# One piece per partition for the loads of the read-out's queries and of the value tile

## The chip, the cores and the metric

The kernel runs on one core of one Trainium2 chip. The metric is the device time of one execution in microseconds (us); the time before is the median of three runs.

## The reference

Three stages follow each other; the change lies in the first. The first stage is a recurrence over 768 steps, run for 4 batches and 8 heads with a state of 40 x 40 each:

```python
for t in range(S):
    y[:, :, t] = np.einsum('bhd,bhde->bhe', rt, state)
    Sa = np.einsum('bhde,bhe->bhd', state, at)
    state = state * wt[:, :, None, :] - np.einsum('bhd,bhe->bhde', Sa, bt) \
            + np.einsum('bhd,bhe->bhde', vt, kt)
```

`y`, laid out as 4 x 768 x 320, goes through a gated feed-forward block (320 to 1024, a convolution of width 3 along the sequence, a sigmoid gate, back to 320), and that result through four attention experts of which each token uses the best two. All of it is float32 in the reference.

## The kernel before, in words

The recurrence is solved in chunks. The sequence is cut into 12 stretches of 64 tokens (`NT`), each into two steps of 32 tokens (`NC`), so 24 steps `k` run one after the other. The 32 head-and-batch pairs are held as `NP = 8` places times four: two halves `al` (or `a`) and two halves `be` (or `b`, `h`). Half of a tile lies on partitions 0 to 63 and the other half on 64 to 127.

Per stretch `prep` works out decays, scaled keys and a triangular inverse `T`. Per step, `chain(k)` forms the corrected values and the new state, and `post(k)` forms the step's read-out. The feed-forward generator `ff` follows them step by step, and `attention` runs after all 24 steps, from about 600 us on.

Four loads per step matter here, all of them issued on SyncE's queue (SP):

- `load_v(k)` fetches the step's values twice: into `SV` (line 138, two loads of 32 partitions, each partition getting two pieces of 320 floats that land next to each other) and into `VZ` (line 143, four loads of 32 partitions, each partition getting eight pieces of 40 floats).
- `load_ra(k)` fetches the read-out's queries `ra` (line 148, two loads of 40 partitions, each partition getting 16 pieces of 32 floats).
- `load_vt(k)` fetches transposed values into `VT` (line 153, two loads, also 16 pieces of 32 floats per partition).
- `load_rb(k)` fetches the same queries in another arrangement into `RB` (line 158, two loads of 40 partitions, each getting one piece of 512 floats).

`VZ` holds the values on partitions 0 to 31 and 64 to 95, and the corrected values, with a minus sign, on partitions 32 to 63 and 96 to 127. The corrected values are written there from PSUM by ScalarE at line 378. Half `be = 0` is filled on the lower partitions only and half `be = 1` on the upper ones only; the rest stays zero. Sixteen matmuls of `chain` (called at line 385, recorded under the helper's line 163) then use `VZ` as the operand that streams past the keys `KB`, 80 columns each. Four copies on ScalarE (line 396) bring the corrected values into `U`. When all of that is done, `load_v(k + 1)` may overwrite `VZ`.

`ra` is the streaming operand, 64 columns each, of sixteen matmuls in `post` (line 444, also recorded under line 163), against `VT`. There is one buffer each of `SV`, `VZ`, `ra`, `VT` and `RB`, so each load waits until the readers of the step before have finished.

The order: `run` merges the generators into one program order by due times written into their `yield`s. From this program order, the tile framework's planner sets the order on each engine and queue, with modelled times (`schedule_with_timeline_sim=True`). Each engine then runs its own list in order, SP too: an SP load that waits for a semaphore holds back every load listed behind it. Besides the loads named, SP issues the loads of `w`, `a` and `kb` (lines 120, 126, 131), the copies of `F` into `a` (line 233), of `KB` and `S` into `LB` (lines 423, 425), the stores of `xe` into `xs` (line 470), the weight loads of the feed-forward block (line 498) and its output (line 634).

Of the kernel before, what the change touches and what calls it, by code (L numbers as in the profile page):

```python
# [8 lines left out]
F32 = mybir.dt.float32  # L9
# [3 lines left out]
AF = mybir.ActivationFunctionType  # L13
# [8 lines left out]
NP, NC = 8, 2  # L22
# [3 lines left out]
R = (slice(0, 40), slice(64, 104))  # L26
Z = (slice(0, 64), slice(64, 128))
E = slice(0, 104)
# [21 lines left out]
class Kernel:  # L50
# [7 lines left out]
    def setup_a(self, ctx):  # L58
        tc, nc = self.tc, self.nc
        cp = self.cp = ctx.enter_context(tc.tile_pool(name="acst", bufs=1))  # L60
        self.wk = ctx.enter_context(tc.tile_pool(name="awk", bufs=2))
        self.w = cp.tile([128, 32, 32], F32, name="w")
        self.kb = cp.tile([128, 16, 2, 2, 32], F32, name="kb")

        self.a = [cp.tile([128, 2, 2, 16, 32], F32, name=f"a{j}") for j in range(2)]
        self.SV = cp.tile([128, 2, 2, NP, 40], F32, name="SV")
        self.ra = cp.tile([128, NP, 2, 2, 32], F32, name="ra")

        self.LB = [cp.tile([128, 2, NP, 2, 40], F32, name=f"LB{j}") for j in range(2)]
        self.RB = cp.tile([128, 2, NP, 2, 32], F32, name="RB")  # L70
        self.P = [cp.tile([128, 32, 32], F32, name=f"P{j}") for j in range(3)]

        self.U = [cp.tile([128, NP // 2, 104], F32, name=f"U{j}") for j in range(2)]
        self.VZ = cp.tile([128, NP, 2, 2, 40], F32, name="VZ")
        self.VT = cp.tile([128, NP, 2, 64], F32, name="VT")
        self.sT = [cp.tile([128, NP, 104], F32, name=f"sT{j}") for j in range(2)]
        self.S = [cp.tile([128, NP, 2, 40], F32, name=f"S{j}") for j in range(2)]
        self.g21 = cp.tile([128, 8, 2, 16], F32, name="g21")
        self.d1 = cp.tile([128, 8, 32], F32, name="d1")
        self.M1 = cp.tile([128, 8, 2, 16], F32, name="M1")  # L80
        self.po = self.ps[3][:, 1].rearrange("p (a b) -> p a b", a=2)
        nc.vector.memset(self.w[32:64], 1.0)
        nc.gpsimd.memset(self.kb[32:64], 0.0)
        nc.gpsimd.memset(self.a[0][32:64], 0.0)
        nc.vector.memset(self.P[0][:, :, 0:1], 1.0)
        nc.vector.memset(self.po[:, 1], 0.0)
        nc.vector.memset(self.ps[1][:, 1, 256:], 0.0)
        cst = cp.tile([128, 164], F32, name="cst")
        self.ident, self.mask = cst[:, :128], cst[:, 128:160]
        self.m0, self.m1, self.m2 = cst[:, 160:161], cst[:, 161:162], cst[:, 162:163]  # L90
        self.cst = cst
        self.t = {}
        self.work = self.nn = 0
# [39 lines left out]
    def load_v(self, k):  # L133

        nc, i = self.nc, self.i
        for al in range(2):
            o = 64 - 64 * al
            nc.sync.dma_start(self.SV[o:o + 32, al].rearrange("p b u d -> p b (u d)"),
                              i["v4"][k].rearrange("(b a t) x -> a t b x", b=2, a=2)[al])
        for h in range(2):  # L140
            for al in range(2):
                v = i["v4"][k, 64 * h + 32 * al:64 * h + 32 * al + 32].rearrange("p (u d) -> p u d", d=40)
                nc.sync.dma_start(self.VZ[64 * h:64 * h + 32, :, al, h], v)

    def load_ra(self, k):

        for h in range(2):
            self.nc.sync.dma_start(self.ra[R[h], :, :, h], self.i["ra"][k, 40 * h:40 * h + 40].rearrange(
                "p (u b t) -> p u b t", u=NP, b=2))

    def load_vt(self, k):
        for h in range(2):
# [180 lines left out]
    def chain(self, k):  # L333
        nc, wk, t = self.nc, self.wk, self.t[k // NC]
        U, KB, u0 = self.U[k % 2], t["KB"], NP * (k % NC)
        zero = k == 0
        sT, sN = self.sT[k % 2], self.sT[(k + 1) % 2]

        def st(x):
            y = x[E]  # L340
            return bass.AP(tensor=y.tensor, offset=y.offset, ap=[list(y.ap[0]), [104, NP], [64, 2], [1, 40]])

        So, SV = self.S[k % 2], self.SV

        def back(p0):
            Sp = self.ps[3][:, 0].rearrange("p (m x) -> p m x", m=4)
            for p in range(4):
                self.tr(WR, Sp[E, p, :104], sT[E, p0 + p], self.ident[:104, :104])
            nc.scalar.activation(So[E, p0:p0 + 4], Sp[E].rearrange("p m (a e) -> p m a e", a=2)[:, :, :, :40], AF.Copy)

        cu = self.ps[0]
        Xp = cu[:, 0, :320].rearrange("p (m d) -> p m d", m=NP)
        for p in range(NP):
            for al in range(2):
                for be in range(2):
                    q = 32 * (2 * be + al)
                    r = slice(0, 96 + 8 * al)
                    self.mm(XA, Xp[q:q + 32, p], t["a"][r, be, al, u0 + p], SV[r, al, be, p], start=True, stop=True)
            if p == 3:
                yield 0.06  # L360
        X = wk.tile([128, NP, 40], F32, name="X", bufs=1)
        nc.scalar.activation(X, Xp, AF.Copy)
        yield 0.14
        if not zero:
            back(0)
            yield 0.25
        for p in range(NP):
            for al in range(2):
                for be in range(2):
                    q = 32 * (2 * be + al)  # L370
                    s, o = slice(q, q + 32), 64 * be + 32
                    self.mm(WX, cu[o:o + 32, al, p * 40:p * 40 + 40], t["T"][s, u0 + p], X[s, p], start=True, stop=True)
        VZ = self.VZ
        for be in range(2):
            s = slice(64 * be + 32, 64 * be + 64)
            y = VZ[s, :, :, be].rearrange("p m a d -> p a m d")
            z = cu[s, :, :320].rearrange("p a (m d) -> p a m d", m=NP)
            nc.scalar.activation(y, z, AF.Copy, scale=-1.0)
        yield 0.4
        if not zero:  # L380
            back(4)
            yield 0.5
        for p in range(NP):
            for al in range(2):
                self.mm(WD, cu[R[al], p // 4, 80 * (p % 4):80 * (p % 4) + 80], KB[:, u0 + p, al],
                        VZ[:, p, al].rearrange("p b d -> p (b d)"), start=True, stop=True)
        for be in range(2):
            s = slice(64 * be + 32, 64 * be + 64)
            for r in range(2):
                y, z = U[64 * r + 32 * be:64 * r + 32 * be + 32], VZ[s, r::2, :, be]  # L390
                y = bass.AP(tensor=y.tensor, offset=y.offset, ap=[list(y.ap[0]), [104, NP // 2], [64, 2], [1, 40]])
                if UD:
                    for al in range(2):
                        nc.sync.dma_start(U[64 * r + 32 * be:64 * r + 32 * be + 32, :, 64 * al:64 * al + 40], VZ[s, r::2, al, be])
                else:
                    nc.scalar.activation(y, z, AF.Copy)
        qq = t["q0"][E, u0:u0 + NP, :, None].to_broadcast([104, NP, 2, 40])
        for h in range(2):
            ps = slice(4 * h, 4 * h + 4)
            Dv = cu[E, h, :320].rearrange("p (m b d) -> p m b d", m=4, b=2)  # L400
            if zero:
                nc.vector.tensor_tensor(st(sN)[:, ps], Dv, qq[:, ps], op=ALU.mult)
            else:
                nc.vector.tensor_tensor(st(sN)[:, ps], Dv, st(sT)[:, ps], op=ALU.add)
        if not zero:
            nc.vector.tensor_tensor(st(sN), st(sN), qq, op=ALU.mult)
        if k + 1 < NT * NC:
            for al in range(2):
                y = sN[R[al]]
                y = bass.AP(tensor=y.tensor, offset=y.offset, ap=[list(y.ap[0]), [64, 2], [104, NP], [1, 40]])  # L410
                nc.gpsimd.tensor_copy(SV[R[al], al], y) if al < SC else nc.scalar.activation(SV[R[al], al], y, AF.Copy)
        if k + 1 < NT * NC:
            self.load_v(k + 1)
        yield 1.0

    def post(self, k):
        nc, wk, t = self.nc, self.wk, self.t[k // NC]
        n, c = divmod(k, NC)
        P, VT = t["P"], self.VT
        ra, LB, RB, u0 = self.ra, self.LB[k % 2], self.RB, NP * c  # L420
# [19 lines left out]
        for p0 in range(0, NP, 4):  # L440
            ap = po(p0, 0).rearrange("p (u a t) -> p u a t", u=4, a=2)
            for p in range(4):
                for be in range(2):
                    self.mm(WA, ap[64 * be:64 * be + 64, p], VT[E, p0 + p, be], ra[E, p0 + p, be], start=True, stop=True)
            for be in range(2):
                s = slice(64 * be, 64 * be + 64)
                y = RB[s, be, p0:p0 + 4].rearrange("p u a t -> p (u a) t")
# [583 lines left out]
```

## Time and profile before

| | before |
|---|---|
| median of 3 runs | 901.09 us (898.76 to 907.43) |
| the profiled execution | 902.53 us |
| its span, first to last instruction | 900.8 us |
| mean granted TensorE clock | 0.929 |
| TensorE (PE) busy | 756.9 us, 84% |
| VectorE (DVE) busy | 699.4 us, 78% |
| ScalarE (ACT) busy | 571.3 us, 63% |
| GpSimd (POOL) busy | 365.6 us, 41% |

Shares are of the span. DMA-issuing instructions on SP don't count as busy; "SPq" in the chain of waits is time in which the chain runs through SP's issuing. The chain of work that ended last is followed back from the last instruction, at each step to what released it. The span lies 1.7 us below the profiled execution's own time. The 24 steps and the feed-forward block fill about the first 600 us, the attention the rest.

### The profile page before, as it was taken

What the parts mean: (1) busy time and instruction counts of PE and PEld (TensorE: products, weight loads), DVE (VectorE), ACT (ScalarE), POOL (GpSimd) and SP (SyncE); (2) the same over time, 40 slices, a digit from 0 to 9 for tenths busy, and PEclk for the clock granted to TensorE, in tenths of its full rate; (3) what the DMA queues carried; (4) which work ended last, traced back from release to release, by engine and by line L of the source; (5) the groups of instructions that cost most, each with busy time, mean ns of one, the idle gap of its engine ahead of it and who ended that gap; (6) DMA issues with size and microseconds to landing.
All of it is one profiled execution on the core that took longest, in us unless ns stands there. A gap on an engine that the chain in (4) does not pass through costs nothing.

```text
span 900.8 us, 31560 instructions
## 1 busy us (share of the span) xinstructions
PE 756.9 (84%) x13112; PEld 659.8 (73%) x13112; DVE 699.4 (78%) x1614; ACT 571.3 (63%) x1353; POOL 365.6 (41%) x419
## 2 busy tenths in 40 slices
PE   1257667988889988898988889959889989999988
PEld 1156556777778877787877779858778878888876
DVE  6888698798798989899898794656567776786664
ACT  1156556676676748584857577657767666776665
POOL 6163443434333324344333235564434353344353
PEclk9999568998898889998998899979999999999999
DMA  5434574545454556553646355250011100110001
GB/s 128 105 121 115 139 170 106 132 101 136 104 132 113 122 130 146 120 128 77 146 108 152 68 121 118 48 143 28 10 45 37 45 16 31 37 38 16 17 15 37
DMA packets 143488, 81.17 MB, mean 90 GB/s; under 512 B 113858, under 2 KB 127042, under 8 KB 142386
## 3 DMA queue, kind: packets, MB, share of 16 engines
q1 hardware_dynamic: 138450, 74.34, 33.8%
q0 software_dynamic: 4896, 4.83, 2.4%
q8 instruction: 103, 1.69, 0.8%
q14 instruction: 39, 0.32, 0.1%
HBM read 51.63 MB, written 11.80 MB: 70 GB/s over the span
## 4 chain that ended last, share of the span: by engine, by line
PE 38%; DVE 29%; ACT 10%; DMA 9%; issue 6%; POOL 4%; SPq 3%; POOLq 0%; ACTq 0%; DVEq 0%
PE ps L163 8%; PE ps L720 4%; DVE cv L604 4%; PE ps L823 4%; PE ps L569 4%; PE ps L806 4%; PE ps L592 3%; PE ps L167 2%; PE ps L770 2%; DVE RB L448 2%; PE ps L711 2%; DVE Q L200 2%; PE ps L838 2%; PE ps L771 2%; DVE a L211 2%
## 5 line engine op out<-in xcount | busy, mean ns | idle before, releaser
L792 POOL TENSOR_TENSOR A<-A,rs 128x128 f32<-128x128 f32 (+5 forms) x96 | 87.7, 936 | 106.3 <-DVE rs L790 61.3
L607 POOL TENSOR_TENSOR cv<-cv,h 128x512 f32<-128x512 f32 (+1 forms) x48 | 59.1, 1230 | 150.0 <-ACT cv L606 129.0
L604 DVE SCALAR_TENSOR_TENSOR cv<-h,cw,cv 128x256 f32<-128x256 f32 (+1 forms) x192 | 97.1, 546 | 25.0 <-ACT cv L602 21.9
L569 PE MATMUL ps<-xh,win 128*128 128x256 f32 x384 | 94.3, 302 | 5.8 <-ACT xh L545 4.2
L569 PE MATMUL ps<-xl,win 128*128 128x256 f32 x384 | 95.1, 300 | 0.5 <-POOL xl L546 0.4
L592 PE MATMUL ps<-wout,gh 128*128 128x320 f32 x384 | 90.5, 331 | 5.8 <-ACT gh L486 5.5
L777 ACT ACTIVATE A<-ps,nm 128x128 f32<-128x128 f32 (+5 forms) x96 | 60.8, 634 | 35.8 <-DVE nm L775 26.8
L487 POOL TENSOR_TENSOR gl<-cv,gh 128x512 fp32r<-128x512 f32 x48 | 62.6, 1305 | 44.6 <-ACT gh L486 44.0
L569 PEld LDWEIGHTS ps<-xh,win 128*128 128x128 f32 x384 | 71.3, 204 | 7.9 <-ACT xh L545 4.7
L592 PEld LDWEIGHTS ps<-wout,gh 128*128 128x128 f32 x384 | 66.2, 201 | 8.3 <-ACT gh L486 6.8
L569 PEld LDWEIGHTS ps<-xl,win 128*128 128x128 f32 x384 | 70.9, 202 | 1.8 <-POOL xl L546 0.8
L775 DVE TENSOR_REDUCE nm<-ps 128x1 f32<-128x128 f32 (+5 forms) x96 | 58.6, 619 | 16.9 <-PE ps L773 10.8
L163 PE MATMUL ps<-kb,a 40*32 40x64 f32 x1536 | 39.2, 254 | 32.7 <-DVE kb L207 29.4
L592 PE MATMUL ps<-wout,gl 128*128 128x320 f32 x192 | 59.4, 332 | 0.9 <-POOL gl L487 0.9
L163 PE MATMUL ps<-RB,LB 104*40 104x32 f32 (+1 forms) x1536 | 50.6, 213 | 11.1 <-DVE RB L448 6.9
L163 PEld LDWEIGHTS ps<-kb,a 40*32 40x32 f32 x1536 | 30.9, 129 | 37.6 <-issue 19.2
L163 PEld LDWEIGHTS ps<-RB,LB 104*40 104x40 f32 (+1 forms) x1536 | 42.2, 127 | 20.5 <-DVE RB L448 9.0
L720 PE MATMUL ps<-x,wqk 128*128 128x384 f32 x256 | 54.5, 353 | 2.8 <-DVE lg L714 2.4
L606 ACT ACTIVATE cv<-cv 128x512 f32<-128x512 f32 (+1 forms) x48 | 30.3, 630 | 39.8 <-DVE cv L604 39.5
L806 PE MATMUL ps<-cid,A 128*128 128x128 f32 x336 | 53.0, 277 | 2.2 <-POOL A L792 1.5
L770 PE MATMUL ps<-k,q 128*128 128x256 f32 (+3 forms) x144 | 49.5, 352 | 3.6 <-ACT A L777 3.3
L163 PE MATMUL ps<-ra,VT 104*64 104x64 f32 x768 | 43.8, 255 | 8.4 <-DVE RB L448 6.8
(178 smaller groups left out, 2177.7 us busy)
## 6 DMA issues: line engine op xcount, KB each, us to landing
kb<-in_kb_e_dram SPq DMA_DIRECT2D x24, 320.0 KB
LB<-KB SPq DMA_DIRECT2D x48, 160.0 KB
LB<-S SPq DMA_DIRECT2D x46, 100.0 KB
a<-in_a_e_dram SPq DMA_DIRECT2D x24, 160.0 KB
VT<-in_vt_dram SPq DMA_DIRECT2D x48, 80.0 KB
RB<-in_rb_dram SPq DMA_DIRECT2D x48, 80.0 KB
SV<-in_v_dram SPq DMA_DIRECT2D x48, 80.0 KB
VZ<-in_v_dram SPq DMA_DIRECT2D x96, 40.0 KB
```

The costliest lines, as they stand in the source:

```text
L163: self.nc.tensor.matmul(*a, **k)
L487: (eng or self.nc.vector).tensor_tensor(lo, x, hi.bitcast(F32), op=ALU.subtract)
L569: nc.tensor.matmul(hp[:, dd], wt[:, 128 * d:128 * d + 128], x, start=k == 0, stop=k == 7)
L592: nc.tensor.matmul(self.ps[1][:, tb, :DM], x, wt, start=d == 0 and k == 0, stop=d == 7 and k == 2)
L604: nc.vector.scalar_tensor_tensor(y, h[:, dd, :, k:k + nt], self.cw[:, k, d:d + 1], y, op0=ALU.mult, op1=ALU.add)
L607: (nc.gpsimd if GM and st % GM == 0 and st >= GN else nc.vector).tensor_tensor(cv[:, :, :, :nt], cv[:, :, :, :nt], h[:, :, :, 1:1 + nt], o ...
L720: nc.tensor.matmul(pp, self.wqk[:, wk, hl, 128 * m:128 * m + 128], x[:, xk], start=j == 0, stop=j == 7)
L770: nc.tensor.matmul(sp[:, c0:c1], q[:, ce, 128 * j:128 * j + 128], k[:, ce, c0:c1], start=True, stop=False)
L775: nc.vector.tensor_reduce(nm, sp[:, :nk], axis=AX.X, op=ALU.max, negate=True)
L777: nc.scalar.activation(A[:, :nk], sp[:, :nk], AF.Exp, bias=nm, accum_out=sums[:, e:e + 1])
L792: nc.gpsimd.tensor_tensor(A[:, :nk], A[:, :nk], rs[:, e:e + 1].to_broadcast([128, nk]), op=ALU.mult)
L806: nc.tensor.transpose(tp[:, m, e], As[e][:, 128 * (2 * g + m):128 * (2 * g + m) + 128], self.cid)
```

## The change

`ra` and `VZ` get another order of axes. In `ra` the half `h` (the one that a load fills) becomes the outermost axis within a partition, so that the 512 floats that a load brings to a partition lie next to each other. In `VZ` the half `be` becomes the outermost axis, then `al`, then the place; one load per half now brings both `al`, two runs of 320 floats of the source that land side by side. Four loads of `VZ` become two. The two matmul groups read the same numbers as before, but each of their streaming operands is now two runs (2 x 40 floats in `VZ`, 2 x 32 in `ra`) where it was one run of 80 or 64. The write at line 378 and the reads at line 396 follow the new order. A branch under `if UD:` is dropped; `UD` is 0, so it never ran.

```diff
-        self.ra = cp.tile([128, NP, 2, 2, 32], F32, name="ra")
+        self.ra = cp.tile([128, 2, NP, 2, 32], F32, name="ra")
...
-        self.VZ = cp.tile([128, NP, 2, 2, 40], F32, name="VZ")
+        self.VZ = cp.tile([128, 2, 2, NP, 40], F32, name="VZ")
...
         for h in range(2):
-            for al in range(2):
-                v = i["v4"][k, 64 * h + 32 * al:64 * h + 32 * al + 32].rearrange("p (u d) -> p u d", d=40)
-                nc.sync.dma_start(self.VZ[64 * h:64 * h + 32, :, al, h], v)
+            nc.sync.dma_start(self.VZ[64 * h:64 * h + 32, h].rearrange("p a u d -> p a (u d)"),
+                              i["v4"][k, 64 * h:64 * h + 64].rearrange("(a t) x -> t a x", a=2))
...
         for h in range(2):
-            self.nc.sync.dma_start(self.ra[R[h], :, :, h], self.i["ra"][k, 40 * h:40 * h + 40].rearrange(
-                "p (u b t) -> p u b t", u=NP, b=2))
+            self.nc.sync.dma_start(self.ra[R[h], h].rearrange("p u b t -> p (u b t)"), self.i["ra"][k, 40 * h:40 * h + 40])
...
-            y = VZ[s, :, :, be].rearrange("p m a d -> p a m d")
+            y = VZ[s, be]
...
-                        VZ[:, p, al].rearrange("p b d -> p (b d)"), start=True, stop=True)
+                        VZ[:, :, al, p], start=True, stop=True)
...
-                y, z = U[64 * r + 32 * be:64 * r + 32 * be + 32], VZ[s, r::2, :, be]
+                y, z = U[64 * r + 32 * be:64 * r + 32 * be + 32], VZ[s, be, :, r::2].rearrange("p a m d -> p m a d")
...
-                    self.mm(WA, ap[64 * be:64 * be + 64, p], VT[E, p0 + p, be], ra[E, p0 + p, be], start=True, stop=True)
+                    self.mm(WA, ap[64 * be:64 * be + 64, p], VT[E, p0 + p, be], ra[E, :, p0 + p, be], start=True, stop=True)
```

## Rows read from the trace of the kernel before

**Rows 1.** The page: busy time per engine, and the chain's shares by engine.

```profile
PE 756.9 (84%) x13112; PEld 659.8 (73%) x13112; DVE 699.4 (78%) x1614; ACT 571.3 (63%) x1353; POOL 365.6 (41%) x419
PE 38%; DVE 29%; ACT 10%; DMA 9%; issue 6%; POOL 4%; SPq 3%; POOLq 0%; ACTq 0%; DVEq 0%
```

**Rows 2.** Busy time by stretch, with granted clock, DMA share and GB/s last.

```profile
360.00:420.00 60.00, 50.40 (x1197) 45.24 (x1199) 55.15 (x113) 38.81 (x87) 23.42 (x24) 0.98 0.52 121
600.00:900.00 300.00, 279.29 (x2249) 240.37 (x2248) 200.92 (x584) 196.24 (x529) 123.45 (x149) 0.98 0.10 32
```

**Rows 3.** SP's issues by line: min/median/max ns, first and last start us.

```profile
L148 SPq DMA_DIRECT2D ra<-in_ra_dram x48: 763/800/4026, 13.8 to 562.5; - x48
L158 SPq DMA_DIRECT2D RB<-in_rb_dram x48: 281/300/1217, 6.9 to 571.4; - x48
L143 SPq DMA_DIRECT2D VZ<-in_v_dram x96: 560/607/1607, 10.4 to 552.2; - x96
L138 SPq DMA_DIRECT2D SV<-in_v_dram x48: 324/392/1602, 9.1 to 539.5; - x48
L153 SPq DMA_DIRECT2D VT<-in_vt_dram x48: 763/764/3974, 6.1 to 565.5; - x48
```

**Rows 4.** Chain in order of time (start, us, what): the issues of ra.

```profile
124.13 1.58 SPq L148
125.76 0.79 SPq L148
...
281.76 0.84 SPq L148
...
282.65 0.82 SPq L148
...
345.93 0.76 SPq L148
...
346.74 0.76 SPq L148
```

**Rows 5.** The chain again: issues of VT after those of ra, longest one last.

```profile
126.59 0.81 SPq L153
...
347.55 3.52 SPq L153
```

**Rows 6.** The chain again: first and last of four VZ issues, a fifth, its landing.

```profile
425.07 0.61 SPq L143
...
427.06 0.60 SPq L143
...
534.48 0.52 SPq L143
535.00 0.05 issue
535.05 2.19 DMA VZ<-in_v_dram
```

**Rows 7.** Matmuls by tile: min/median/max ns; a scattered streaming operand, then a contiguous one.

```profile
L163 PE MATMUL ps<-O,g x768: 209/228/258, 48.5 to 538.6; 32*32 32x32 f32 x192
L163 PE MATMUL ps<-M,d x768: 184/191/258, 53.3 to 542.1; 32*32 32x32 f32 x192
```

**Rows 8.** ScalarE by line: busy us, mean ns, idle before.

```profile
L378 ACT ACTIVATE VZ<-ps 32x640 f32<-32x640 f32 x48 | 33.4, 697 | 15.8 <-PE ps L163 14.8
L630 ACT ACTIVATE yt<-ps 128x640 f32<-128x640 f32 x12 | 8.4, 698 | 0.6 <-PE ps L592 0.5
L396 ACT ACTIVATE U<-VZ 32x320 f32<-32x320 f32 x96 | 44.9, 468 | 1.6
L362 ACT ACTIVATE X<-ps 128x320 f32<-128x320 f32 x24 | 10.3, 430 | 5.5 <-PE ps L163 5.5
```

**Rows 9.** The page's DMA part: packets by size, and the SP queue's share.

```profile
DMA packets 143488, 81.17 MB, mean 90 GB/s; under 512 B 113858, under 2 KB 127042, under 8 KB 142386
q1 hardware_dynamic: 138450, 74.34, 33.8%
```

**Rows 10.** SP's own waits: us in total, times, longest us.

```profile
SPq L158 <- PE ps L163: 26.5, 14, 5.0
SPq L143 <- PE ps L163: 19.5, 12, 9.3
SPq L148 <- PE ps L167: 9.2, 3, 5.7
```

More of the change, by code (lines that the diff above doesn't have):

```diff
@@ L389, in chain @@
             for r in range(2):
-                y, z = U[64 * r + 32 * be:64 * r + 32 * be + 32], VZ[s, r::2, :, be]
+                y, z = U[64 * r + 32 * be:64 * r + 32 * be + 32], VZ[s, be, :, r::2].rearrange("p a m d -> p m a d")
                 y = bass.AP(tensor=y.tensor, offset=y.offset, ap=[list(y.ap[0]), [104, NP // 2], [64, 2], [1, 40]])
[L392 to L396, printed above, removed]
+                nc.scalar.activation(y, z, AF.Copy)
         qq = t["q0"][E, u0:u0 + NP, :, None].to_broadcast([104, NP, 2, 40])
```

## Prediction

> **What bounds the kernel now.** I read the page's busy times first, then the busy times by stretch, then the chain of waits, then SP's issues and waits. No engine is full: TensorE is busy for 84% of the span and VectorE for 78% [rows 1]. In a stretch in the middle of the 24 steps TensorE works 50.4 of 60 us and VectorE 55.15, and the DMA engines are busy for 0.52 of it; in the attention, after 600 us, the DMA share is 0.10 [rows 2]. The first two thirds are a lockstep of engines, and their length is set by the chain that runs through them. That chain is 38% TensorE, 29% VectorE, 9% transfers and 3% SP's issuing [rows 1]: 3% of 900.8 us is some 27 us. The change touches loads of the first 600 us only, and it touches arithmetic nowhere. So its worth has to be sought in those 3%, in the part of the 9% that belongs to its loads, and against that in what the new operand shapes cost TensorE and ScalarE.
>
> **What the loads cost SP now.** An `ra` issue holds SP for a median of 0.800 us and there are 48; a `VZ` issue holds it for 0.607 us and there are 96 [rows 3]. That is 38.4 + 58.3 = 96.7 us of SP, or 4.0 us for each of the 24 steps; from first to last `ra` load it is 548.7 us [rows 3], so a step takes about 23.9 us.
>
> After the change an `ra` load has the shape of today's `RB` load: 40 partitions, one piece of 512 floats each. Its price is a row: 0.300 us [rows 3]. A `VZ` load has the shape of today's `SV` load: 32 partitions, two source runs of 320 floats that land as one. That price is 0.392 us [rows 3], and there are 48 of them, not 96. New sum: 14.4 + 18.8 = 33.2 us. SP is relieved of 63.5 us, 2.6 us per step. Most of this is hidden, since SP's work lies beside that of TensorE and VectorE and only 27 us of all SP issuing stands on the chain. What counts is where these loads stand on it.
>
> **The `ra` issues on the chain.** There are six pieces, 1.58 + 0.79 + 0.84 + 0.82 + 0.76 + 0.76 = 5.55 us [rows 4]. At 0.30 us each they would be 1.8 us: a gain of 3.75 us. Bounds: 0, if another chain of equal length stands beside it, and 5.55, if the loads leave the chain.
>
> **The `VZ` issues on the chain.** Four in a row, between 0.61 and 0.60 us, about 2.4 us in all, and a single one of 0.52 us [rows 6]. The four become two of 0.392, the one becomes 0.392: 2.4 + 0.52 - 0.78 - 0.39 = 1.7 us gained. Bounds 0 and 2.9. Behind the single one stands the landing of that load, 2.19 us [rows 6]; its bytes stay the same, so I take nothing for it, with a bound of half, 1.1 us.
>
> **The queue behind them.** `VT` stays as it is, and its issue has a median of 0.764 us, yet one on the chain took 3.52 us, straight behind two `ra` issues [rows 3, 5]. An issue that takes four times its median was held up by what was already queued. The two `ra` loads ahead of it bring 2 x 640 pieces now and 2 x 40 afterwards. Bounds: nothing, since `VT` itself makes 640 pieces per load, and 2.75 us (down to the median). It is as near to the one as to the other, so I take half: 1.4 us.
>
> **The transfers.** A step's `ra` and `VZ` loads make 2 x 40 x 16 + 4 x 32 x 8 = 2,304 pieces now, all under 512 bytes, and 2 x 40 + 2 x 64 = 208 after; over 24 steps 55,296 become 4,992. The page counts 113,858 packets under 512 bytes [rows 9], so some 58,600 remain. What this saves the DMA engines is bounded by nothing (the bytes are the same) and by 50,304 packets at the SP queue's mean. That mean is 0.338 x 16 x 900.8 us / 138,450 = 35 ns [rows 9], which gives 1,770 us over 16 engines, 111 us of each or 12 points of the share. Small pieces carry few bytes, so I go near the lower end: the queue's share falls from 33.8% to 30 or 32%. With engines about half busy [rows 2], I take no gain on the chain for it beyond the one above.
>
> **TensorE.** Two groups of 16 matmuls per step, 768 each in all, get a streaming operand of two runs instead of one. No row shows two runs. The nearest rows are a pair of the same size: with 32 single floats apart from each other the median is 228 ns, with 32 side by side 191 ns [rows 7]. The difference, 37 ns for 31 extra jumps, is the upper bound for one extra jump: 1,536 x 37 ns = 57 us of TensorE. The lower bound is nothing. In proportion to the jumps it is 1.2 ns each, 1.8 us in all; with TensorE holding 38% of the chain [rows 1] that is 0.7 us lost. I take that, since one jump in 64 or 80 columns is far nearer to a contiguous read than to a scattered one.
>
> **ScalarE.** The write at line 378 becomes contiguous: 697 ns now, and a contiguous write of 640 floats from PSUM takes 698 ns [rows 8], so nothing changes. The reads at line 396 keep runs of 40 floats: 468 ns against 430 for a contiguous copy of 320 floats from PSUM [rows 8]. At worst the difference moves by as much again, 38 ns x 96 = 3.6 us of an engine that holds 10% of the chain, 0.4 us. I take nothing.
>
> **The sum.** -3.75 - 1.7 - 1.4 + 0.7 = -6.2 us. Against the profiled execution's own 902.5 us (span 900.8 and 1.7 around it) that is 896.3. This execution lies 1.4 us above the median of the runs, 901.09, so the median after should be 895.
>
> **A rule against it.** Four issues of `VZ` at 2.4 us stand on the chain, and the one landing of `VZ` on it took 2.19 us [rows 6]: SP's time is as long as the transfer's. The Trainium skill, "DMA: Bandwidth & Descriptors", section "Issuing engines are not separate DMA queues", says that the sequencer's time to initiate a DMA is usually small relative to the DMA itself. By this rule shorter issuing would be worth next to nothing and the time would stay at 901; these rows disagree with it.
>
> **The rivals.**
>
> *Hidden anyway, 899 to 902.* The relieved 63.5 us are off the chain, and where they are on it a neighbouring chain is as long. For it: in the middle stretch VectorE is busy for 92% [rows 2], so a load that comes 1 us earlier finds VectorE still at work. Against it: eleven pieces of these loads stand on the chain as it is [rows 4, 6]. Chance 0.25.
>
> *The queue was the brake, 884 to 890.* SP runs its list in order, so 2.6 us less per step shortens the delay of every load and copy behind: `LB`, `xs`, `a`, `RB`. All of the issuing of `ra`, `VZ` and `VT` in these rows and the half landing would go: 5.55 + 2.9 + 4.3 + 1.1 = 13.9 us [rows 4 to 6], so 887. For it: the 3.52 us stall. Against it: SPq is but 3% of the chain. Chance 0.24.
>
> *SP stands at a closed door, 906 to 918.* SP already waits for TensorE before `RB`, `VZ` and `ra` loads for 26.5, 19.5 and 9.2 us, up to 9.3 us at a time [rows 10], because their single buffers are still being read. Fewer and shorter loads, planned anew, can put a `VZ` load ahead of work that is ready, `xs` or `LB` copies and the feed-forward input behind them; SP then waits at `VZ` while they are late. The three rows make 55.2 us, 2.3 us per step. It decides from 0.26 us more per step (6.2 / 24, the gain is gone); 0.65 us more, a growth by under a third, makes 895 + 24 x 0.65 = 911. For it: the order on SP is a planned one, and it will differ. Against it: two waits fewer per step, as four `VZ` issues become two. Chance 0.13.
>
> *Two runs are dear, 909 to 920.* If an extra jump costs as much as the scattered operand, 57 us of TensorE at 38% is 22 us: 895 - 0.7 + 22 = 916. It decides from about 10 ns per matmul (1,536 x 10 ns x 0.38 = 5.8 us, the gain). For it: nothing shows a two-run operand. Against it: the proportion above. Chance 0.05.
>
> **How the numbers follow.** My own forecast, 895 with a range of 889 to 899, has 0.33. Within 1% is about what a measurement of this kernel can tell from no change: 892.1 to 910.1. Faster than that: all of the braked queue (0.24) and a quarter of my own case (0.08), together 0.32. Slower: a good half of the closed door (0.08) and nearly all of the dear runs (0.04), 0.12. The rest is 0.56. The range reaches from the braked queue's 884 to the smaller half of the closed door at 910; outside lie a fifth of the former, half of the latter and most of the dear runs, under 0.2. Both signs hold much of it, so my own case's range stands beside it above.
>
> **What would show it.** `ra` issues at a median near 0.30 us and 48 `VZ` issues near 0.39; packets under 512 bytes near 58,600; `ra` and `VZ` matmuls within 5 ns of now; line 378 near 697 ns; SPq on the chain down to 2%, and lines 148 and 143 gone from it or under 1 us a piece. The forecast is wrong if SP's waits for TensorE grow by 16 us or more, if the two matmul groups grow by 10 ns or more, or if the chain through VectorE and TensorE comes out longer although the loads behave as forecast: then the new plan, and not the loads, has set the time.

## The result, and the profile after

The changed kernel takes 915.87 us (median of 4 runs, 912.76 to 917.98) against 902.86 us for the kernel before (4 runs, 898.76 to 907.43). The ratio is 1.0135, with an interval from 1.0091 to 1.0179: it became slower by 1.35%. (Ratios here and below leave out a slower state into which some executions of any of these kernels fall, and aren't the quotient of the medians.) The profiled execution took 915.1 us, of which 913.3 are its span.

The page of the changed kernel (busy time by engine, the DMA packets, the SP queue, the chain's shares by engine), to be held against [rows 1, 9]:

```profile
PE 755.2 (83%) x13112; PEld 659.1 (72%) x13112; DVE 708.0 (78%) x1614; ACT 567.9 (62%) x1351; POOL 372.3 (41%) x419
...
DMA packets 92416, 81.17 MB, mean 89 GB/s; under 512 B 57794, under 2 KB 74050, under 8 KB 91314
q1 hardware_dynamic: 87378, 74.33, 31.1%
...
PE 32%; DVE 31%; ACT 12%; DMA 10%; issue 9%; POOL 5%; SPq 1%; ACTq 0%; DVEq 0%; POOLq 0%
```

TensorE works as long as before and SP's issuing has all but left the chain (3% to 1%), yet the span is 12.5 us longer. Next SP's issues of the loads in the changed kernel (min/median/max ns, first and last start in us), which answer to [rows 3]. Line 147 is `ra` (148 before), line 141 `VZ` (143), line 151 `VT` (153):

```profile
L147 SPq DMA_DIRECT2D ra<-in_ra_dram x48: 281/323/1237, 13.6 to 579.4; - x48
...
L141 SPq DMA_DIRECT2D VZ<-in_v_dram x48: 312/416/1768, 10.2 to 570.9; - x48
...
L151 SPq DMA_DIRECT2D VT<-in_vt_dram x48: 763/822/1100, 6.1 to 581.5; - x48
```

The loads became as short as forecast, and the longest `VT` issue fell from 3.97 to 1.10 us. So the place of the loss is elsewhere. Cutting the time at the first `VZ` matmul of step 10 and at that of step 23 (steps counted from 0) finds it. The busy times by stretch of the kernel before (columns: TensorE, weight loads, VectorE, ScalarE, GpSimd, then granted clock, DMA share, GB/s); first everything between the two cuts, then the feed-forward matmuls of lines 569 and 592 alone, then everything after the second cut:

```profile
282.70:565.10 282.40, 249.36 (x5827) 223.02 (x5823) 240.66 (x490) 197.57 (x435) 104.69 (x113) 0.93 0.52 119
...
282.70:565.10 282.40, 65.72 (x416) 57.58 (x416) 0.93 0.52 119
...
282.70:565.10 282.40, 53.75 (x291) 45.18 (x291) 0.93 0.52 119
...
565.10:900.80 335.70, 307.50 (x2588) 265.79 (x2582) 223.01 (x621) 216.33 (x578) 148.36 (x171) 0.98 0.13 37
```

The same four rows of the changed kernel (the feed-forward lines are now 563 and 586):

```profile
281.90:585.10 303.20, 258.56 (x5895) 231.85 (x5895) 252.03 (x499) 201.77 (x450) 112.48 (x115) 0.92 0.44 111
...
281.90:585.10 303.20, 65.25 (x432) 57.55 (x432) 0.92 0.44 111
...
281.90:585.10 303.20, 65.51 (x313) 54.17 (x312) 0.92 0.44 111
...
585.10:913.30 328.20, 297.84 (x2460) 255.91 (x2460) 213.49 (x607) 207.19 (x554) 141.24 (x165) 0.97 0.12 36
```

Up to step 10 the two are level (281.9 against 282.7 us). Then thirteen steps take 303.2 us where they took 282.4, 20.8 us more. After the second cut the changed kernel is 7.5 us quicker (328.2 against 335.7). That adds up: -0.8 + 20.8 - 7.5 = 12.5 us, the growth of the span. The 20.8 us are two things. TensorE does 9.2 us more work there; the feed-forward matmuls have grown by 65.25 + 65.51 - 65.72 - 53.75 = 11.3 us, that is, some of them were brought forward. And TensorE idles 11.6 us longer (303.20 - 258.56 = 44.6 against 282.40 - 249.36 = 33.0). The first part comes back after the loop, where TensorE has 307.50 - 297.84 = 9.7 us less to do. The idling doesn't come back.

What TensorE waits for between the cuts, kernel before (us in total, times, longest):

```profile
PE ps L163 <- DVE RB L448: 10.7, 9, 2.6
...
PE ps L163 <- DVE T L330: 4.2, 2, 2.4
PE ps L163 <- DVE xe L463: 3.3, 3, 1.7
...
PE ps L167 <- ACT KB L267: 1.2, 4, 0.5
```

And in the changed kernel:

```profile
PE ps L161 <- DVE RB L442: 14.5, 8, 3.7
...
PE ps L165 <- ACT KB L265: 5.8, 7, 1.7
PE ps L161 <- DVE xe L457: 5.7, 3, 2.9
...
PE ps L161 <- DVE T L328: 1.0, 2, 0.6
```

TensorE waits 3.8 us longer for VectorE's write of `RB`, 4.6 us longer for ScalarE's `KB`, 2.4 us longer for `xe`, and 3.2 us less for `T`. These are other engines' arithmetic, none of it touched by the change, and no load of the change is among them. It is what a different order of the same work would look like. In fact 5,943 of the 8,168 places in TensorE's list hold another instruction than before. (The trace has more records than the list has places: a step's 16 matmuls on `VZ` stand in it as 32, so each group of 768 records is 384 matmuls.) The question for the experiments was whether that order is the cause, or whether the loads brought the loss about in some other way.

### The profile page after: what moved, and what is told of

The parts are those of the page before. It is cut to its first block, busy times and chain, and to the rows that moved or that the text cites. A ratio compares the mean times of both kernels' runs of the same rounds, so it can differ in the third digit from the quotient of the medians.

```text
span 913.3 us, 31465 instructions
## 1 busy us (share of the span) xinstructions
PE 755.2 (83%) x13112; PEld 659.1 (72%) x13112; DVE 708.0 (78%) x1614; ACT 567.9 (62%) x1351; POOL 372.3 (41%) x419
## 2 busy tenths in 40 slices
DMA packets 92416, 81.17 MB, mean 89 GB/s; under 512 B 57794, under 2 KB 74050, under 8 KB 91314
## 3 DMA queue, kind: packets, MB, share of 16 engines
q1 hardware_dynamic: 87378, 74.33, 31.1%
## 4 chain that ended last, share of the span: by engine, by line
PE 32%; DVE 31%; ACT 12%; DMA 10%; issue 9%; POOL 5%; SPq 1%; ACTq 0%; DVEq 0%; POOLq 0%
DVE cv L598 6%; PE ps L161 4%; PE ps L714 4%; PE ps L817 4%; PE ps L800 3%; DMA xs<-xe 2%; PE ps L705 2%; PE ps L586 2%; DVE RB L442 2%; DVE a L209 2%; PE ps L764 2%; DMA kb<-in_kb_e_dram 2%; PE ps L563 2%; DVE Q L198 2%; PE ps L832 2%
## 5 line engine op out<-in xcount | busy, mean ns | idle before, releaser
L598 DVE SCALAR_TENSOR_TENSOR cv<-h,cw,cv 128x256 f32<-128x256 f32 (+1 forms) x192 | 96.9, 542 | 35.5 <-ACT cv L596 34.8
L601 POOL TENSOR_TENSOR cv<-cv,h 128x512 f32<-128x512 f32 (+1 forms) x48 | 62.5, 1303 | 144.6 <-ACT cv L600 144.1
L586 PE MATMUL ps<-wout,gh 128*128 128x320 f32 x384 | 95.6, 344 | 2.1 <-ACT gh L480 2.1
L771 ACT ACTIVATE A<-ps,nm 128x128 f32<-128x128 f32 (+5 forms) x96 | 60.8, 634 | 37.4 <-DVE nm L769 28.4
L586 PEld LDWEIGHTS ps<-wout,gh 128*128 128x128 f32 x384 | 69.8, 211 | 4.1 <-ACT gh L480 3.1
L161 PE MATMUL ps<-kb,a 40*32 40x64 f32 x1536 | 37.8, 250 | 32.4 <-DVE kb L205 29.9
L586 PE MATMUL ps<-wout,gl 128*128 128x320 f32 x192 | 62.0, 345 | 0.7 <-POOL gl L481 0.6
L161 PEld LDWEIGHTS ps<-RB,LB 128*40 128x40 f32 (+1 forms) x1536 | 41.1, 125 | 24.6 <-DVE RB L442 11.4
```

Source lines behind the costliest of these rows:

```text
L161: self.nc.tensor.matmul(*a, **k)
L586: nc.tensor.matmul(self.ps[1][:, tb, :DM], x, wt, start=d == 0 and k == 0, stop=d == 7 and k == 2)
L598: nc.vector.scalar_tensor_tensor(y, h[:, dd, :, k:k + nt], self.cw[:, k, d:d + 1], y, op0=ALU.mult, op1=ALU.add)
L601: (nc.gpsimd if GM and st % GM == 0 and st >= GN else nc.vector).tensor_tensor(cv[:, :, :, :nt], cv[:, :, :, :nt], h[:, :, :, 1:1 + nt], o ...
L771: nc.scalar.activation(A[:, :nk], sp[:, :nk], AF.Exp, bias=nm, accum_out=sums[:, e:e + 1])
```

## The experiments

**The tool.** The planner chooses the order of each engine's list anew for each program. To part layout from order, the list of each engine was written out from one kernel and forced on another by edges that only order issue:

```diff
         Kernel(tc, ins, {"out": out}).run()
+        follow(tc, nc, ORDER)
...
+            if was is not None:
+                tc.add_manual_dep(seq[e][n], was.name, info, reason="order")
+            was = seq[e][n]
```

`ORDER` is the list of places per engine. No arithmetic changes.

### Layout and order apart

The changed kernel in the order of the kernel before; its edit is the one above, in the changed kernel:

> Both new layouts and the two new load shapes, but every engine and SP's queue issue their instructions in the order of the kernel before (a VZ load takes the place of the first of the two that it replaces). Theory A, the planner's new order costs the time and the loads by themselves are worth what I forecast: 888 to 901 us, under the kernel before. Rival B, the loads or the two-run operands cost the time whatever the order: 912 to 918 us.

Measured: 900.94 us, ratio 0.9963 [0.9921, 1.0006]. The loss is gone with the order. The same kernel was run once more, in five rounds, to tell half a per cent from nothing:

> New layouts in the order of the kernel before once more, for the size of what the loads are worth when the order stays. My sum of -6.2 us gives a ratio of 0.993 to the kernel before; nothing gained gives 1.000; the earlier run gave 0.996.

Measured: 898.67 us against 904.75, ratio 0.9951 [0.9920, 0.9982]. This version beats both kernels. Its busy time by stretch between the same two cuts:

```profile
276.50:558.80 282.30, 250.77 (x5835) 224.68 (x5825) 240.19 (x490) 198.12 (x436) 106.00 (x113) 0.93 0.48 119
```

And two of TensorE's waits there:

```profile
PE ps L161 <- DVE RB L442: 9.0, 8, 2.6
...
PE ps L165 <- ACT KB L265: 0.4, 1, 0.4
```

The thirteen steps are back at 282.3 us, TensorE's idling at 31.5 us, and the wait for `KB` is down from 5.8 to 0.4 us. The granted clock, 0.93 of full speed here and 0.92 in the changed kernel, is too near to make 20.8 us: if all of TensorE's 258.56 us went with it, 0.01 would be some 2.8 us (an estimate).

The cross-check is the old layouts in the order of the changed kernel (the same edit in the kernel before, with the other list):

> The layouts and loads of the kernel before, issued in the order of the changed kernel (each VZ load as two, one behind the other). Theory A: 914 to 925 us, as slow as the changed kernel or slower by the loads' worth. Rival B: 899 to 905 us.

Measured: 923.74 us, ratio 1.0242 [1.0158, 1.0326]. With the layouts untouched, the new order costs more than the whole change did. The matmuls on `VZ`, by tile, in this kernel (min/median/max ns, first and last start us):

```profile
L163 PE MATMUL ps<-VZ,KB x768: 231/233/357, 63.3 to 595.9; 128*40 128x80 f32 x192
```

Its last `VZ` matmul starts at 595.9 us, later than in any kernel so far. Between the first `VZ` matmul of step 10 and that of step 23 it shows

```profile
283.40:593.90 310.50, 265.70 (x5893) 238.45 (x5894) 251.73 (x497) 202.43 (x449) 112.44 (x115) 0.89 0.47 108
```

The four corners by ratio: old layouts in the old order 1, new layouts in the old order 0.995, old layouts in the new order 1.024, new layouts in the new order 1.0135. The order costs 1.9 to 2.4% with either layout. In the old order the layouts gain 0.5%. In the new order they would gain 1%, but the intervals of the two overlap, and the kernel with the old layouts had a mean granted clock of 0.89 there against 0.92 in the changed kernel: TensorE was busy for 7.1 us longer (265.70 against 258.56) with the same matmuls. So the size of their gain in the new order stays open.

### Each part alone, planned anew

The `ra` part of the diff alone, and the `VZ` part alone, the planner free:

```diff
-        self.ra = cp.tile([128, NP, 2, 2, 32], F32, name="ra")
+        self.ra = cp.tile([128, 2, NP, 2, 32], F32, name="ra")
```

> Only ra's layout and load are changed; the planner orders anew. Rival B: the effects of the two parts add up to some +13 us, so this one lies between 898 and 916 and with the VZ part makes the whole. Theory A: no such sum need come out, as each program has an order of its own; within 890 to 920.

Measured: 919.95 us, ratio 1.0198 [1.0123, 1.0274]. That lies above what the adding of parts allowed (898 to 916).

```diff
-        self.VZ = cp.tile([128, NP, 2, 2, 40], F32, name="VZ")
+        self.VZ = cp.tile([128, 2, 2, NP, 40], F32, name="VZ")
```

> Only VZ's layout and loads are changed; the planner orders anew. Rival B: this and the ra part add up to some +13 us over the kernel before. Theory A: they need not; within 890 to 920.

Measured: 916.19 us, ratio 1.0167 [1.0086, 1.0248]. Each half of the change alone costs as much as the whole, within the intervals. Two costs that belonged to the parts would have had to add up.

### Edits that mean nothing

If a new plan is enough to lose a per cent, an edit that does no harm by itself may lose it too. One kernel loads a table of constants a second time at the start, the other clears three tiles in the reverse sequence:

```diff
+        nc.sync.dma_start(self.cst, self.i["consts"])
```

> The kernel before with one load of the constants issued twice at its start: no layout and no load of the loop is touched, some 0.5 us of work is added before the first step, and the planner orders anew (5,183 of TensorE's 8,168 matmuls get another place in its list). Theory A', the order of the kernel before is an uncommonly good one and nearly any new plan is worse: 908 to 925 us. Rival C, the plan gets worse because of the shorter loads: 898 to 907 us.

Measured: 914.26 us, ratio 1.0155 [1.0093, 1.0218]. 5,183 of TensorE's 8,168 places differ from the kernel before.

```diff
-        for t in (self.SV, self.VZ, self.d1):
+        for t in (self.d1, self.VZ, self.SV):
```

> The kernel before with three memsets of the start in another order: not a load, a layout or an operation more or less; 5,922 of TensorE's 8,168 matmuls get another place in its list. Theory A': 908 to 925 us. Rival C: 898 to 907 us.

Measured: 913.43 us, ratio 1.0119 [1.0033, 1.0205]; 5,922 places differ. The `VZ` matmuls of the kernel with the second load of constants:

```profile
L164 PE MATMUL ps<-VZ,KB x768: 229/233/356, 64.4 to 577.6; 128*40 128x80 f32 x192
```

One more load before the first step can't delay the last step by 11.4 us (577.6 against 566.2) by its own length: the first `VZ` matmul starts only 1.2 us later (64.4 against 63.2). Five programs planned anew (the change, its halves, the two empty edits) lie between 1.0119 and 1.0198. So the order that the planner happened to find for the kernel before is better than the five others seen here.

### Where in the loop, and whether on SP

Three kernels with the new layouts put the two orders one after the other. The old order until step 10 and the new one from there:

> New layouts; the order of the kernel before up to the corrected values of step 10, from there the order of the changed kernel. If the loss is made after step 10, as the traces show (the two run level until there): 912 to 920 us. If it is made before: 898 to 905 us.

Measured: 917.51 us, ratio 1.0180 [1.0117, 1.0244]. The mirror of it, the new order until step 10 and then the old:

> New layouts; the order of the changed kernel up to the corrected values of step 10, from there the order of the kernel before. Loss made after step 10: 897 to 905 us. Loss made before: 911 to 918 us. Both this and its mirror near 908: the loss is spread evenly.

Measured: 896.36 us, ratio 0.9963 [0.9926, 1.0000]. And the old order until step 16, then the new:

> New layouts; the order of the kernel before up to the corrected values of step 16, from there the order of the changed kernel. If the loss of the new order is spread evenly over steps 10 to 23: about 908 us. If it lies in one place between step 10 and 16: 898 to 904 us; after step 16: 912 to 918 us.

Measured: 911.38 us, ratio 1.0073 [1.0033, 1.0113]. The `VZ` matmuls of the first, and of its mirror:

```profile
L161 PE MATMUL ps<-VZ,KB x768: 229/233/356, 62.6 to 587.2; 128*40 128x80 f32 x192
```

```profile
L161 PE MATMUL ps<-VZ,KB x768: 230/233/356, 61.6 to 554.6; 128*40 128x80 f32 x192
```

The new order costs nothing in the first ten steps and everything after them: the last step starts at 587.2 or at 554.6 us, depending on the second part alone. All of these kernels, and the one with the old order throughout, are forced by the same kind of edges, so the forcing isn't what parts them. (The changed kernel's own order wasn't forced on it; old until step 10 and then new comes near it, 917.51 against 915.87 us.)

With the cut at step 16 about half of the loss is left by the ratios (0.995, 1.007, 1.018). 911.38 us lies between the forecasts for an even loss (908) and for a loss after step 16 (from 912 on), and the runs scatter from 903.81 to 916.69. The traces speak for uneven steps. From the first `VZ` matmul of step 16 to that of step 23 the kernel before, the changed kernel and this one show

```profile
423.50:565.10 141.60, 127.85 (x2974) 114.60 (x2972) 116.01 (x236) 101.22 (x223) 54.38 (x58) 0.94 0.52 116
```

```profile
428.30:585.10 156.80, 137.27 (x3138) 123.54 (x3131) 128.35 (x254) 109.17 (x245) 63.44 (x63) 0.93 0.43 109
```

```profile
422.70:584.70 162.00, 138.28 (x3094) 124.77 (x3092) 125.30 (x251) 109.22 (x245) 63.80 (x64) 0.94 0.42 105
```

So 15.2 of the changed kernel's 20.8 us fall on the steps from 16 on, and 5.6 on steps 10 to 15 (146.4 us against 140.8). The profiled execution of this kernel, one of its longest at 915.14 us, has 20.4 us from step 16 on.

The rival of the prediction that named a new plan had placed it on SP. So one kernel took the new order on the four computing engines but SP's list from the old one (346 of 592 places differ):

> New layouts, the order of the changed kernel on TensorE, VectorE, ScalarE and GpSimd, but SP issues its loads and copies in the order of the kernel before (346 of 592 places differ). My rival of the closed door, that SP's new list puts loads that must wait ahead of work that is ready, gives 898 to 905 us. If the loss is in the order of the computing engines: 912 to 919 us.

Measured: 929.69 us, ratio 1.0275 [1.0222, 1.0329]. That is outside both forecasts. SP's old list doesn't bring the time back; with the engines in another order it costs more. Since this kernel, too, mixes lists of two plans, the time alone can't clear SP's new list, and the mirror (old lists on the engines, SP's new one) wasn't run.

The traces speak against it. The work that SP would hold up by this rival includes the stores of `xe` into `xs`, from which GpSimd fetches the feed-forward input. GpSimd does wait longer for them between the cuts, kernel before and changed kernel:

```profile
POOL xd L537 <- DMA xs<-xe: 8.0, 5, 3.6
```

```profile
POOL xd L531 <- DMA xs<-xe: 18.9, 9, 4.7
```

But it isn't SP that is late. From the last write to `xe` to the start of a stretch's first store, the twelve stretches take 6.8 us in all in the kernel before (2.85 us at most) and 1.8 us in the changed kernel (0.53 at most). The stores leave almost as soon as `xe` is there. The copies of `S` into `LB`, too, follow the last write to `S` sooner (133.5 us in sum over 46 copies, against 192.0). What comes late is `xe`, or GpSimd comes early; SP doesn't hold that work back. That leaves the lists of the computing engines, though no run shows them by themselves.

### One that settled little

The recurrence in the old order, with the feed-forward instructions in the places that the new order gives them, was to show whether bringing those forward is the harm:

> New layouts. The instructions of the feed-forward generator stand where the changed kernel's order has them among all others; everything else keeps among itself the order of the kernel before. If the new order is slow because it puts feed-forward work ahead of the recurrence from step 10 on: 911 to 919 us. If it is slow by the order within the recurrence and its preparation: 896 to 904 us. In between: both.

Measured: 974.52 to 1003.51 us in five runs, ratio 1.0779 [1.0676, 1.0883]. That is far above both orders, so the kernel doesn't lie between them and can't say which part of the new order costs what. It shows only how much an order may cost that fits neither plan. Its mirror, and kernels that swap the list of TensorE or VectorE alone, weren't run.

The last start of a `VZ` matmul beside the span of the same profiled execution, over all of these but the last:

| kernel | last `VZ` matmul (us) | span (us) |
|---|---|---|
| before | 566.2 | 900.8 |
| new layouts, old order; the same in five rounds | 555.8; 559.9 | 892.1; 897.1 |
| new layouts, new order until step 10, then old | 554.6 | 889.0 |
| changed kernel | 587.0 | 913.3 |
| old layouts, new order | 595.9 | 920.9 |
| `ra` alone; `VZ` alone | 589.8; 584.6 | 915.2; 915.5 |
| constants twice; tiles cleared in reverse | 577.6; 578.0 | 911.1; 910.4 |
| old order until step 10; until step 16, then new | 587.2; 586.6 | 915.6; 913.3 |
| new order, SP's list from the old one | 602.0 | 928.7 |

Whatever loses time has its last step late, and more so than its span; in the changed kernel that is because part of the delay is work brought forward. The others agree: of 1,344 records of feed-forward matmuls in the trace (lines 569 and 592 before), 316 run after the start of step 23 in the four kernels of the table's first three rows, and 244 to 284 in all of the table's others. The loss doesn't follow their number, though: with 284 left (constants twice) the ratio is 1.0155, with 251 (tiles in reverse) 1.0119.

## Why the prediction was wrong

**The step that failed** is the sum. It added up the loads' costs as if each engine kept its list, and set the new order at nothing. The order was the largest term: +1.9% at fixed layout (from 0.995 to 1.0135), some 17 us, against -6.2 us for everything that was summed. The range lacked it too, and ended at 910. The text named the replanning twice, once in the rival at SP and once in its last sentence, but gave it a price only on SP. Of the signs that it named for being wrong, that last one came out in part: the loads behaved as forecast and the plan set the time, but the chain's share of TensorE and VectorE together fell, from 67 to 63%. ScalarE's, the transfers', GpSimd's and the unexplained ("issue") shares grew.

**The `ra` and `VZ` issues** were priced rightly. 48 x 0.323 + 48 x 0.416 = 35.5 us instead of 96.7, a relief of 61.2 us where 63.5 were forecast. In the changed kernel's chain two pieces of these loads and `VT` are left, both of `VZ` (start, us, what), 1.36 us in all where [rows 4 to 6] have 12.8 without the landing:

```profile
570.50 0.34 SPq L141
...
570.89 1.02 SPq L141
```

The new order has a part in this: with the old layouts in the new order SP's issuing is 1% of the chain too. With the order held (five rounds) 0.86 us of these loads are left on the chain; so some 12 us left it, and the time fell by a third to a half of that.

**The stall of `VT`** became shorter, as forecast: its longest issue is 1.10 us, not 3.97 [rows 3, 5]. It goes with the load of `ra`: the longest `VT` issue takes 3.2 to 4.5 us in the five kernels with the old `ra` load and 0.87 to 2.75 us in those with the new one. But the queue kept its stalls. In the new layouts with the old order (five rounds) an issue of `VZ` takes 3.83 us, where 1.61 was the longest before [rows 3]:

```profile
L151 SPq DMA_DIRECT2D VT<-in_vt_dram x48: 763/816/866, 6.1 to 556.9; - x48
```

```profile
L141 SPq DMA_DIRECT2D VZ<-in_v_dram x48: 312/418/3829, 10.4 to 544.2; - x48
```

And the median of `VT` rose from 0.764 to 0.82 us. That this term was worth its 1.4 us isn't shown.

**The packets** came out as worked out: 57,794 under 512 bytes (forecast 58,600), the queue's share 31.1% (30 to 32).

**TensorE and ScalarE.** Two runs in a streaming operand cost nothing that shows. The matmuls by tile, and ScalarE's write at line 376 (378 before), of the changed kernel:

```profile
L161 PE MATMUL ps<-VZ,KB x768: 230/233/357, 64.0 to 587.0; 128*40 128x80 f32 x192
...
L161 PE MATMUL ps<-ra,VT x768: 216/222/371, 72.9 to 597.5; 104*64 104x64 f32 x192
...
L376 ACT ACTIVATE VZ<-ps x48: 695/697/702, 62.5 to 584.3; 32x640 f32<-32x640 f32 x48
```

Those of the kernel before:

```profile
L163 PE MATMUL ps<-VZ,KB x768: 229/233/357, 63.2 to 566.2; 128*40 128x80 f32 x192
...
L163 PE MATMUL ps<-ra,VT x768: 222/222/370, 72.1 to 579.0; 104*64 104x64 f32 x192
```

The medians stay at 233 and 222 ns, and the write at 697 [rows 8]. The ends of matmuls are modelled in the profile, so their starts are the better test. In an unbroken row of them, matmuls on `VZ` start 37.8 ns after each other before, and 35.0 and 38.4 ns in the two runs of the new layouts with the old order; matmuls on `ra` 31.5 ns before, then 30.9 and 31.5 (each the median over the rows). The rival of the dear runs falls. Its price was no more than a ceiling, as matmuls overlap: the pair of [rows 7] takes 228 and 191 ns, but successive ones start 14 and 9 ns apart.

**The sum with the order held.** 902.5 - 6.2 is a ratio of 0.993; the five rounds gave 0.9951 [0.9920, 0.9982]. So the sum holds the measured value of the layouts, at its generous end: 0.49% of 904.75 is 4.4 us (the two medians lie 6.1 us apart). The queue as the brake (-13.9 us, 0.985) lies outside this interval. So does "hidden anyway" for all but its best value (899 of 901, 0.998). The Trainium skill, "DMA: Bandwidth & Descriptors", section "Issuing engines are not separate DMA queues", which stood against the change, holds that the time to initiate a DMA is usually small beside the DMA itself. Here 61.2 us less issuing is worth 4.4 us, 7% of it, which is closer to that rule than to a queue that sets the time, but not nothing. The prediction said that its rows disagree with the rule, but it set four issues beside one landing; one `VZ` issue took 0.52 to 0.61 us beside a landing of 2.19 us [rows 6].

**The closed door at SP** had the right sign and the right size (906 to 918) for a wrong reason. The test named for it was that SP's waits for TensorE grow by 16 us. Over all that SP issues they grew by 28.4 us, from 124.0 to 152.4, which would have said yes; over the three loads that the rival named, `RB`, `VZ` and `ra`, by 3.6 us, from 69.6 to 73.2. The largest rows before are those of [rows 10] and

```profile
SPq L148 <- PE ps L163: 7.3, 7, 2.5
```

In the changed kernel (`RB`, `VZ`, `ra`):

```profile
SPq L156 <- PE ps L161: 28.0, 13, 7.2
...
SPq L141 <- PE ps L161: 24.2, 9, 6.3
...
SPq L147 <- PE ps L161: 19.3, 8, 5.0
```

In the new layouts with the old order, 892.1 us of span, they read

```profile
SPq L156 <- PE ps L161: 44.4, 14, 7.0
...
SPq L141 <- PE ps L161: 26.2, 10, 8.6
...
SPq L147 <- PE ps L161: 13.4, 8, 4.7
```

There the three loads' waits for TensorE make 91.3 us and those of all that SP issues 160.6: more, in the faster kernel. SP needs less time for its issues and stands longer at the same doors. So here such a wait tells that SP is early, and not that anyone is late. What speaks against the rival itself are the stores of `xe`, which left SP sooner than before, and the time that SP's old list did not bring back (1.0275).

**What stays open.** Why the order of the kernel before is good, and which of the moved instructions does the harm, isn't settled. The feed-forward matmuls that were brought forward go with the loss in every slow order of the table, but the one kernel that moved them alone fitted neither plan.

## What to carry to other kernels

Where a planner orders the lists, a change to any instruction is two changes: what it does, and a new draw of the order. Here the draw was worth 1.2 to 2% and the change itself 0.5%, so a measurement of the pair says little about the change until the order is held fixed or a few empty edits have shown how far draws scatter. An order that turned out well is worth keeping: written out and forced on the changed kernel, it made the version that beats both.

## What the runs showed of the hardware

Merging small packets saved far less than the mean time of a packet. The SP queue moved 138,450 packets before and 87,378 after, at the same bytes. Its time over 16 engines went from 0.338 x 16 x 900.8 = 4,871 us to 0.311 x 16 x 913.3 = 4,545 us. That is 326 us for 51,072 packets, 6.4 ns each, where the mean of that queue was 35 ns [rows 9]. With the old order held the two runs of the new layouts (0.316 of 892.1 and of 897.1 us) give 361 and 335 us, 6.6 to 7.1 ns each.

The pieces of a load don't set the price of its issue alone. `ra` fell from 0.800 to 0.323 us when 640 pieces became 40. But the copies of `S` into `LB`, 40 partitions with one run of 640 floats each, whose source lies on the chip, hold SP for 0.774 us in the kernel before, as long as a scattered load from DRAM [rows 3]:

```profile
L425 SPq DMA_DIRECT2D LB<-S x46: 737/774/832, 84.5 to 559.7; - x46
```

What makes them so dear wasn't tested.
